# Two feed-forward blocks behind a linear-attention layer: where the first part's splits, weight tiles and tables stand

## The chip, the cores and the metric

One core of a Trainium2 chip runs the whole program in one launch. The metric is the device time of that launch in microseconds (us). The kernel before took 898.88 us, the median of three runs (898.12 to 900.89).

## What is computed

The reference, cut to what matters:

```python
# q, k, v: (4, 8, 768, 64)
for t in range(S):                      # S = 768, gamma per head
    state = gamma * state + outer(k[:, :, t], v[:, :, t])
    y[:, :, t] = scale * q[:, :, t] @ state
x = y in rows of (batch, token), 3072 x 512
h = x @ w_in                            # 512 x 2048
x = (h - tanh(h)) @ w_out               # 2048 x 512
h = x @ w_in2                           # 512 x 1024
solu = h * softmax(h)
out = (layernorm(solu) * g_ln) @ w_out2 # 1024 x 512
```

The weights arrive as 64-bit floats, seen as pairs of 32-bit words. The kernel decodes them into a high and a low 32-bit part, and each product of the feed-forward blocks is made of three matmuls (high by high, high by low, low by high).

## The kernel before

**Units.** The attention is worked in chunks of 128 tokens. A unit is one chunk of one batch entry with all its heads; there are 24, six chunks of four entries, and unit k belongs to chunk k // 4. Each unit has two z parts of 512 KB, with q and k in one and k and v in the other (`load_half`, L192).

`prepare` (L213 to L237) makes a unit's scaled q and v in a tile `vq`: GpSimd (POOL) multiplies q by a table of decays (`qs`, L223) and half of the heads of v by constants (L234); ScalarE (ACT) scales the other four heads (L230). The table `tab` is one for each chunk, 256 KB, in two buffers (`load_tab`, L188).

`unit(ko, ks)` (L240 to L316) does two things: the output of unit `ko` and the scores and states of unit `ks`. On TensorE (PE) the output is `out` products from the states `sa`, `sb` and the masked scores `pr`; the scores are `sc` products, which land in the same tile as the state's gain. All of these are 64x64 matmuls at L211. ACT then copies the output to `xf` (L277, or L280 and L281 in the first chunk), VectorE (DVE) adds the second piece (L285), and `split_x` (L318) makes the high part `xh` on ACT (L323) and the low part `xl` on DVE and POOL (L324). For unit `ks`, DVE masks the scores into `pr` (L305), ACT or DVE makes the state `sb` (L311, L313), and DVE makes the next chunk's state `sa` (L316).

**Weight tiles.** A w_in tile is loaded by SyncE (SP) at L120 and decoded in three stages: an Abs on ACT into `wf` (L126), four steps on DVE (L133, L134, L137, L140), and the split into high and low parts `w`, a cast on ACT (L149) and a subtraction on DVE (L150).

**Order.** The first part works the eight units of the first two chunks: units 0 and 1 are prepared and scored, then a loop over k does the output of unit k beside the scores of unit k + 2, with unit k + 3 prepared in the middle (`ahead`). In the last two rounds the first products `ph` of the feed-forward block (L337) join. From there on PE works 128x512 matmuls to the end. Each engine, and SP's queue of loads, works its instructions in order. `pin` keeps an instruction in program order; one that isn't pinned is put where a scheduler sees fit when the program is built. The loads are not pinned.

```python
def load_tab(c):
    tb[c] = stp.tile([P, NP * P], F32, tag="tab", name="tab", bufs=2)
    (nc.sync if c else nc.scalar).dma_start(out=tb[c], in_=tab[c])
```

Of the kernel before, what the change touches and what calls it, by code (L numbers as in the profile page):

```python
# [26 lines left out]
F32 = mybir.dt.float32  # L27
F32R = mybir.dt.float32r
I32 = mybir.dt.int32
AF = mybir.ActivationFunctionType  # L30
# [5 lines left out]
B, H, S, D = 4, 8, 768, 64  # L36
P = 128
# [10 lines left out]
LAG = 2  # L48
LATER = 3
LOADS = 3  # L50
N4, N2 = 44, 15


W_MIN, W_MAX = (
# [7 lines left out]
C_IDENT = C_MASK + D  # L62
# [28 lines left out]
def body(ctx: ExitStack, tc, z, w_in, w_out, w_in2, w_out2, g_ln, cst, tab, out):  # L91
    nc = tc.nc
# [7 lines left out]
    def pin(ins, on=True):  # L100

        if on:
            tc.keep_in_program_order(ins)
# [7 lines left out]
    con = cpool.tile([P, C_IDENT], F32, name="con")  # L111
# [75 lines left out]

    def load_tab(c):  # L188
        tb[c] = stp.tile([P, NP * P], F32, tag="tab", name="tab", bufs=2)
        (nc.sync if c else nc.scalar).dma_start(out=tb[c], in_=tab[c])  # L190

    def load_half(k, half):  # L192
        t = t4([P, 2, NP, P], F32, "z")
        nc.sync.dma_start(out=t.rearrange("p a b c -> p (a b c)"), in_=z[2 * k + half])
        (zv if half else zq)[k] = t

    def load_units(upto):
        while loaded[0] < min(upto, NU):
            k = loaded[0]
            if k // B not in tb:  # L200
                load_tab(k // B)
            for half in range(2):
                load_half(k, half)
            loaded[0] += 1
# [8 lines left out]
    def prepare(k, own, wide=False):  # L213

        c = k // B
        if wide:
            t = t4([P, 2, H * D], F32, "vq")
            v = t[:, 0, :].rearrange("q (h d) -> q h d", h=H)
            qs[k] = t[:, 1, :].rearrange("q (p t) -> q p t", p=NP)
        else:  # L220
            v = t2([P, H, D], F32, "vs")
            qs[k] = t2([P, NP, P], F32, "qs")
        pin(nc.gpsimd.tensor_tensor(  # L223
            qs[k].rearrange("q p t -> q (p t)"),
            zq[k][:, 0, :, :].rearrange("q p t -> q (p t)"), tb[c], ALU.mult,
        ), wide)
        src = zv[k][:, 1, :, :].rearrange("q p (h d) -> q (p h) d", h=2)
        c0 = C_VS + c * H
        for h in range(own):
            pin(nc.scalar.activation(  # L230
                v[:, h, :], src[:, h, :], AF.Copy, scale=con[:, c0 + h : c0 + h + 1]
            ), wide)
        if own < H:
            pin(nc.gpsimd.tensor_tensor(  # L234
                v[:, own:, :], src[:, own:, :],
                con[:, c0 + own : c0 + H].unsqueeze(2).to_broadcast([P, H - own, D]), ALU.mult,
            ), wide)  # L237
        vs[k] = v

    def unit(ko, ks, hold=False, pool=ps_r, tag="r", engs=None, amid=None):  # L240

        if ko is not None:
            c, b = divmod(ko, B)
            q, v, po, st = qs.pop(ko), vs.pop(ko), pt.pop(ko), (sa.pop(ko, None), sb.pop(ko))
            w = [ps_r.tile([P, 2, 4 * D], F32, tag="r", name="out") for _ in range(2)]
            fr = [t[:, 0, :].rearrange("q (i t) -> q i t", i=2) for t in w]
            y = [t[:, 1, :].rearrange("q (h i t) -> q h i t", h=2, i=2) for t in w]  # L250

            steps = range(2) if c else (1,)
            products([
                (
                    fr[h][rows(col(2 * i + odd, h)), i, rows(ab)],
                    st[ab][rows(h), 2 * i + odd, :], q[rows(h), 2 * i + odd, rows(ab)],
                )
                for i in range(2) for ab in steps for odd in range(2) for h in range(2)
            ])
            products([  # L260
                (
                    y[ab][rows(col(p, h)), h, p // 2, :], v[rows(ab), 2 * p + h, :],
                    po[rows(ab), h, p, :],
                )
                for p in range(NP) for ab in range(2) for h in range(2)
            ])
            if hold:
                if b % 2 == 0:
                    xc[b // 2] = t4([P, 2, 2, 2, P], F32, "xc")
                xf = xc[b // 2][:, b % 2, :, :, :]  # L270
            else:
                xf = t2([P, 2, 2, P], F32, "xf")
            xa = xf.rearrange("q h i t -> q (h i) t")
            ya = [t.rearrange("q h i t -> q (h i) t") for t in y]
            if c:
                for h in range(2):
                    pin(nc.scalar.copy(xf[:, h, :, :], fr[h]), amid)  # L277
            else:
                for h in range(2):
                    pin(nc.scalar.copy(xf[:, h, :, rows(1)], fr[h][:, :, rows(1)]), amid)  # L280
                pin(nc.scalar.copy(xa[:, :, rows(0)], ya[0]), amid)  # L281
            if amid:
                amid()
            for ab in steps:
                pin(nc.vector.tensor_tensor(  # L285
                    xa[:, :, rows(ab)], xa[:, :, rows(ab)], ya[ab], ALU.add
                ), amid)
            if not hold:
                split_x(c, b, xf, engs or (nc.gpsimd, nc.gpsimd), amid)
        if ks is not None:  # L290
            c = ks // B
            kt, kv, v, q = zq.pop(ks)[:, 1, :, :], zv.pop(ks), vs[ks], qs[ks]
            w = [pool.tile([P, 2, 4 * D], F32, tag=tag, name="sc") for _ in range(2)]
            sc, gn = ([t[:, n, :].rearrange("q (p t) -> q p t", p=NP) for t in w] for n in range(2))
            products([
                (sc[h][rows(ab), p, :], kt[rows(h), p, rows(ab)], q[rows(h), p, rows(ab)])
                for p in range(NP) for h in range(2) for ab in range(2)
            ])
            products([
                (gn[ab][rows(h), p, :], kv[rows(ab), 0, p, rows(h)], v[rows(ab), 2 * p + h, :])  # L300
                for p in range(NP) for ab in range(2) for h in range(2)
            ])
            pr = t2([P, 2, NP, D], F32, "pr")
            for h in range(2):
                pin(nc.vector.tensor_tensor(  # L305
                    pr[:, h, :, :], sc[h], mask.unsqueeze(1).to_broadcast([P, NP, D]), ALU.mult
                ), amid)
            pt[ks] = pr
            sb[ks] = stp.tile([P, NP, D], F32, tag="sb", name="sb", bufs=3)
            if c == 0:  # L310
                nc.scalar.copy(sb[ks], gn[0])  # L311
            else:
                nc.vector.tensor_tensor(sb[ks], sa[ks], gn[0], ALU.add)  # L313
            if c < NC - 1:
                sa[ks + B] = stp.tile([P, NP, D], F32, tag="sa", name="sa")
                nc.vector.tensor_tensor(sa[ks + B], sb[ks], gn[1], ALU.add)  # L316

    def split_x(c, b, xf, engs, fixed=False):  # L318
        if b == 0:
            xt[c] = [[t4([P, 2, SB], F32R, f"x{n}") for _ in range(2)] for n in "hl"]  # L320
        for h in range(2):
            xh, xl = (xt[c][n][h][:, :, b * P : (b + 1) * P] for n in range(2))
            pin(nc.scalar.copy(xh, xf[:, h, :, :]), fixed)  # L323
            pin(engs[h].tensor_tensor(xl, xf[:, h, :, :], xh.bitcast(F32), ALU.subtract), fixed)  # L324
# [75 lines left out]

    spare = dict(pool=ps_y, tag="y")
    dec1.n = NF1

    warm = cpool.tile([P, 1], F32, name="warm")
    nc.gpsimd.memset(warm, 0.0)
    nc.scalar.activation(warm, warm, AF.Tanh)
    g2 = {}

    def step_h(n, b):
# [3 lines left out]

    load_half(0, 0)
    load_tab(0)
    nc.scalar.dma_start(out=con, in_=cst[:, :C_IDENT])
    load_half(0, 1)
    loaded[0] = 1
    load_units(2)
    dec1.to(0, 2)  # L420
    load_units(2 * B)
    for k in range(2):
        prepare(k, H // 2, True)
        unit(None, k, **spare)
    for st in (1, 2):
        dec1.to(st, 1, True)
    prepare(2, H // 2, True)

    def ahead(k):
# [3 lines left out]
    for k in range(2 * B):  # L433
        both = (nc.vector, nc.gpsimd) if k < 2 * B - 1 else (nc.vector, nc.vector)
        unit(
            k, k + 2 if k + 2 < 2 * B else None, engs=both,
            amid=lambda: ahead(k + 3), **spare
        )

        if k == 0:  # L440
            for st, n in ((3, 1), (1, 2), (2, 2)):
                dec1.to(st, n, True)
        elif k == 1:
            dec1.to(3, 2, True)
        elif k >= 2 * B - 2:
            if k == 2 * B - 1:
                dec1.to(0, 4)
                for st in (1, 2, 3):
                    dec1.to(st, 3, True)
            step_h(k - (2 * B - 2), 0)  # L450
# [241 lines left out]
```

## Time and profile before

| | us |
|---|---|
| median of three runs | 898.88 |
| lowest and highest run | 898.12, 900.89 |
| the profiled execution | 900.99 |
| its span, first to last instruction | 899.2 |
| PE busy | 874.1 |
| DVE busy | 434.1 |
| ACT busy | 301.4 |
| POOL busy | 193.8 |

The span is what the trace covers; the profiled execution's own time has 1.8 us around it. The trace can be read as totals, as busy time in chosen stretches, or as a timeline of one engine's instructions, each with the idle time ahead of it and what ended that. "Issue" there stands for idle time in which the engine waited for nothing that the profile shows. [...]

### The profile page before, as it was taken

What the parts mean: (1) busy time and instruction counts of PE and PEld (TensorE: products, weight loads), DVE (VectorE), ACT (ScalarE), POOL (GpSimd) and SP (SyncE); (2) the same over time, 40 slices, a digit from 0 to 9 for tenths busy, and PEclk for the clock granted to TensorE, in tenths of its full rate; (3) what the DMA queues carried; (4) which work ended last, traced back from release to release, by engine and by line L of the source; (5) the groups of instructions that cost most, each with busy time, mean ns of one, the idle gap of its engine ahead of it and who ended that gap; (6) DMA issues with size and microseconds to landing.
All of it is one profiled execution on the core that took longest, in us unless ns stands there. A gap on an engine that the chain in (4) does not pass through costs nothing.

```text
span 899.2 us, 15890 instructions
## 1 busy us (share of the span) xinstructions
PE 874.1 (97%) x6656; PEld 723.5 (80%) x6656; DVE 434.1 (48%) x873; ACT 301.4 (34%) x606; POOL 193.8 (22%) x200
## 2 busy tenths in 40 slices
PE   4699999999999999999999999999999999999998
PEld 4588888888888887888788888888888888888886
DVE  3679759981232232222222279954444444444442
ACT  4556436550111111111111134523444433333332
POOL 4411000000234333333333200011222212122210
PEclk8799999999999999999999999999999999999999
DMA  9663105340321112111310055114111111100000
GB/s 359 251 265 130 48 1 187 95 140 0 94 95 48 60 64 79 48 47 48 95 48 14 12 183 150 43 41 123 47 48 40 35 44 47 36 24 24 24 24 35
DMA packets 34775, 71.93 MB, mean 80 GB/s; under 512 B 3088, under 2 KB 15504, under 8 KB 34704
## 3 DMA queue, kind: packets, MB, share of 16 engines
q1 hardware_dynamic: 18288, 58.01, 19.0%
q10 hardware_dynamic: 16416, 12.91, 4.5%
q8 instruction: 52, 0.85, 0.4%
q14 instruction: 19, 0.16, 0.1%
HBM read 58.32 MB, written 12.58 MB: 79 GB/s over the span
## 4 chain that ended last, share of the span: by engine, by line
PE 94%; DMA 2%; issue 1%; DVE 1%; ACT 1%; POOL 1%; ACTq 0%; POOLq 0%
PE ph L337 29%; PE py L362 29%; PE po L616 15%; PE ph L568 15%; PE out L211 3%; PE ptr L603 2%; PE sc L211 2%; DMA z<-z 1%; DMA con<-cst 1%; DMA y1d<-ysb 0%; POOL qs L223 0%; POOL vs L234 0%; DVE g L345 0%; ACT th L344 0%; DVE w L150 0%
## 5 line engine op out<-in xcount | busy, mean ns | idle before, releaser
L362 PE MATMUL py<-gh,w 128*128 128x512 f32 x768 | 248.8, 392 | 0.0
L337 PE MATMUL ph<-xh,w 128*128 128x512 f32 x768 | 247.9, 393 | 0.0
L337 PEld LDWEIGHTS ph<-xh,w 128*128 128x128 f32 x768 | 145.3, 189 | 31.0
L362 PEld LDWEIGHTS py<-gh,w 128*128 128x128 f32 x768 | 143.3, 188 | 30.4 <-ACT gh L350 0.2
L345 DVE TENSOR_TENSOR g<-ph,th 128x512 f32<-128x512 f32 x96 | 66.2, 690 | 182.3 <-ACT th L344 182.3
L337 PE MATMUL ph<-xl,w 128*128 128x512 f32 x384 | 150.4, 392 | 0.0
L362 PE MATMUL py<-gl,w 128*128 128x512 f32 x384 | 149.8, 390 | 0.0
L344 ACT ACTIVATE th<-ph 128x512 f32<-128x512 f32 x96 | 57.3, 598 | 258.9 <-PE ph L337 245.9
L568 PE MATMUL ph<-w,y 128*128 128x512 f32 x576 | 134.9, 389 | 0.0
L353 POOL TENSOR_TENSOR gl<-g,gh 128x512 fp32r<-128x512 f32 x48 | 61.9, 1289 | 331.6 <-DVE gh L352 298.0
L568 PEld LDWEIGHTS ph<-w,y 128*128 128x128 f32 x576 | 108.0, 188 | 22.4
L616 PE MATMUL po<-w,uh 128*128 128x512 f32 x384 | 120.4, 395 | 0.0
L397 POOL TENSOR_TENSOR y<-yl,y 128x512 fp32r<-128x512 f32 x24 | 42.2, 1761 | 260.9 <-ACT y L396 260.9
L574 DVE TENSOR_REDUCE nmx<-ph 128x1 f32<-128x1024 f32 x24 | 29.4, 1225 | 117.7 <-PE ph L568 117.7
L337 PEld LDWEIGHTS ph<-xl,w 128*128 128x128 f32 x384 | 72.6, 189 | 14.9
L362 PEld LDWEIGHTS py<-gl,w 128*128 128x128 f32 x384 | 72.1, 188 | 14.9
L616 PEld LDWEIGHTS po<-w,uh 128*128 128x128 f32 x384 | 70.6, 188 | 13.6
L616 PE MATMUL po<-w,ul 128*128 128x512 f32 x192 | 75.3, 392 | 0.0
L577 ACT ACTIVATE ex<-ph,nmx 128x1024 f32<-128x1024 f32 x24 | 26.8, 1117 | 132.5 <-DVE nmx L574 132.5
L579 DVE SCALAR_TENSOR_TENSOR ex<-ph,ex 128x1024 f32<-128x1024 f32 x24 | 29.4, 1225 | 29.8 <-ACT ex L577 29.8
L616 PEld LDWEIGHTS po<-w,ul 128*128 128x128 f32 x192 | 36.0, 188 | 7.6
L353 DVE TENSOR_TENSOR gl<-g,gh 128x512 fp32r<-128x512 f32 x48 | 33.8, 707 | 10.1 <-PE py L362 8.1
(76 smaller groups left out, 840.4 us busy)
## 6 DMA issues: line engine op xcount, KB each, us to landing
z<-z SPq DMA_DIRECT2D x48, 512.0 KB, 5.3
raw<-w_in SPq DMA_DIRECT2D x24, 512.0 KB, 5.2
raw<-w_out SPq DMA_DIRECT2D x24, 512.0 KB, 3.7
y1d<-ysb ACTq DMA_DIRECT2D x24, 256.0 KB, 3.5
yl<-y1d SPq DMA_DIRECT2D x24, 256.0 KB, 3.2
out<-ob ACTq DMA_DIRECT2D x24, 256.0 KB, 2.2
tab<-tab SPq DMA_DIRECT2D x5, 256.0 KB, 2.6
tab<-tab ACTq DMA_DIRECT2D x1, 256.0 KB, 4.7
```

Of the source, the lines that this page charges most:

```text
L211: pin(nc.tensor.matmul(o, a, b, start=True, stop=True, skip_group_check=True))
L337: nc.tensor.matmul(ph, a[:, k, :], x, start=n == 0, stop=n == 3 * NK - 1), s < 2
L344: nc.scalar.activation(th, ph, AF.Tanh)
L345: nc.vector.tensor_tensor(g, ph, th, ALU.subtract)
L353: eng_l.tensor_tensor(gl_, g, gh.bitcast(F32), ALU.subtract)
L362: nc.tensor.matmul(py[e], a[:, cols], x, start=f == 0 and n == 0, stop=f == NF1 - 1 and n == 2)
L397: nc.gpsimd.tensor_tensor(yo, t, yh.bitcast(F32), ALU.subtract)
L568: nc.tensor.matmul(ph[:, half, :], a[:, k, :], b, start=n == 0, stop=n == 3 * NK - 1)
L574: nc.vector.tensor_reduce(nmx, phf, AX.X, ALU.max, negate=True)
L577: nc.scalar.activation(ex, phf, AF.Exp, bias=nmx, scale=1.0, accum_out=ssum)
L579: nc.vector.scalar_tensor_tensor(ex, phf, 1.0, ex, ALU.mult, ALU.mult, accum_out=us)
L616: nc.tensor.matmul(po, a[:, f, :], b, start=n == 0, stop=n == 3 * NF2 - 1)
```

## The change

Five things change, all in the first part:

- `split_x` of unit k (the making of `xh` and `xl`) is called behind the scores and states of unit k + 2, at the end of `unit`, instead of ahead of them.
- The first two w_in tiles are loaded directly behind unit 0's two z parts, ahead of unit 1's, and decoded around unit 1's scores: tile 0 between the scores of units 0 and 1, tile 1 behind them. Before, they were decoded ahead of and inside the loop's first two rounds.
- The loads of the tables are pinned, so they stay in program order on SP.
- The load of the constants is pinned and stands ahead of the tiny activation that loads ACT's table.
- ACT's copy of the first chunk's `sb` is pinned.

```diff
@@ load_tab
-        (nc.sync if c else nc.scalar).dma_start(out=tb[c], in_=tab[c])
+        pin((nc.sync if c else nc.scalar).dma_start(out=tb[c], in_=tab[c]))
@@ unit
-            if not hold:
-                split_x(c, b, xf, engs or (nc.gpsimd, nc.gpsimd), amid)
+            if not hold and not amid:
+                split_x(c, b, xf, engs or (nc.gpsimd, nc.gpsimd))
...
             if c == 0:
-                nc.scalar.copy(sb[ks], gn[0])
+                pin(nc.scalar.copy(sb[ks], gn[0]))
             else:
                 nc.vector.tensor_tensor(sb[ks], sa[ks], gn[0], ALU.add)
             if c < NC - 1:
                 sa[ks + B] = stp.tile([P, NP, D], F32, tag="sa", name="sa")
                 nc.vector.tensor_tensor(sa[ks + B], sb[ks], gn[1], ALU.add)
+        if amid:
+            split_x(*divmod(ko, B), xf, engs, True)
@@ body
-    warm = cpool.tile([P, 1], F32, name="warm")
-    nc.gpsimd.memset(warm, 0.0)
-    nc.scalar.activation(warm, warm, AF.Tanh)
...
     load_half(0, 0)
     load_tab(0)
-    nc.scalar.dma_start(out=con, in_=cst[:, :C_IDENT])
+    pin(nc.scalar.dma_start(out=con, in_=cst[:, :C_IDENT]))
     load_half(0, 1)
+
+    warm = cpool.tile([P, 1], F32, name="warm")
+    nc.gpsimd.memset(warm, 0.0)
+    pin(nc.scalar.activation(warm, warm, AF.Tanh))
     loaded[0] = 1
-    load_units(2)
     dec1.to(0, 2)
     load_units(2 * B)
-    for k in range(2):
-        prepare(k, H // 2, True)
-        unit(None, k, **spare)
-    for st in (1, 2):
-        dec1.to(st, 1, True)
+    prepare(0, H // 2, True)
+    unit(None, 0, **spare)
+    for st, n in ((1, 1), (2, 1), (1, 2)):
+        dec1.to(st, n, True)
+    prepare(1, H // 2, True)
+    dec1.to(3, 1, True)
+    unit(None, 1, **spare)
+    for st in (2, 3):
+        dec1.to(st, 2, True)
     prepare(2, H // 2, True)
...
-        if k == 0:
-            for st, n in ((3, 1), (1, 2), (2, 2)):
-                dec1.to(st, n, True)
-        elif k == 1:
-            dec1.to(3, 2, True)
-        elif k >= 2 * B - 2:
+        if k >= 2 * B - 2:
```

How the order of the built program moves, at three places. The first is SP's queue of loads, up to the weight tiles behind the second chunk's z parts; `tab` are the tables (the load of the first one stands on ACT). Before:

```order
L194 DMA z<-z 128x1024 x4
L120 DMA raw<-w_in 128x1024 x2
L194 DMA z<-z 128x1024 x4
L190 DMA tab<-tab 128x512
L194 DMA z<-z 128x1024 x8
L451 DMA gl<-g_ln 128x8
L557 DMA ident<-cst 128x128
L190 DMA tab<-tab 128x512 x2
L120 DMA raw<-w_in 128x1024 x5
L194 DMA z<-z 128x1024 x4
L120 DMA raw<-w_in 128x1024
```

With the change:

```order
L194 DMA z<-z 128x1024 x2
L120 DMA raw<-w_in 128x1024 x2
L194 DMA z<-z 128x1024 x6
L190 DMA tab<-tab 128x512
L194 DMA z<-z 128x1024 x8
L451 DMA gl<-g_ln 128x8
L557 DMA ident<-cst 128x128
L120 DMA raw<-w_in 128x1024 x5
L190 DMA tab<-tab 128x512
L194 DMA z<-z 128x1024 x4
L120 DMA raw<-w_in 128x1024
```

The two w_in tiles now pass unit 1's z parts. Of the two tables that stood ahead of five w_in tiles, the one of chunk 2 stands behind them and the one of chunk 3 has gone further down, behind the last w_out tile.

The second place is ACT, from unit 0's scaling to unit 2's. `vq_127` is unit 0's; unit 1's is `vq_175` before and `vq_183` with the change; unit 2's is `vq_229` and `vq_241`. Before:

```order
L230 ACTIVATE vq_127<-z_91,con_69 128x64 x4
L311 COPY sb_171<-sc_134 128x256
L230 ACTIVATE vq_175<-z_95,con_69 128x64 x4
L311 COPY sb_219<-sc_182 128x256
L126 ACTIVATE wf_223<-raw_97 128x512
L230 ACTIVATE vq_229<-z_103,con_69 128x64 x4
```

With the change:

```order
L230 ACTIVATE vq_127<-z_88,con_69 128x64 x4
L311 COPY sb_171<-sc_134 128x256
L126 ACTIVATE wf_175<-raw_93 128x512
L126 ACTIVATE wf_181<-raw_95 128x512
L230 ACTIVATE vq_183<-z_99,con_69 128x64 x4
L149 CAST w_190<-wf_175 128x512
L311 COPY sb_230<-sc_193 128x256
L149 CAST w_238<-wf_181 128x512
L230 ACTIVATE vq_241<-z_103,con_69 128x64 x4
```

Both tiles' Abs and both casts now stand ahead of unit 2's scaling.

The third place is DVE, from unit 0's state to unit 2's scores (`pr_316` before, `pr_320` with the change). Before:

```order
L316 TENSOR_TENSOR sa_173<-sb_171,sc_135 128x256
L305 TENSOR_TENSOR pr_216<-sc_182,con_69 128x256
L305 TENSOR_TENSOR pr_216<-sc_183,con_69 128x256
L316 TENSOR_TENSOR sa_221<-sb_219,sc_183 128x256
L133 TENSOR_SCALAR wf_223<-wf_223 128x512
L134 TENSOR_SCALAR wf_223<-wf_223 128x512
L137 SCALAR_TENSOR_TENSOR wf_223<-raw_97,wf_223 128x512
L140 SCALAR_TENSOR_TENSOR wf_223<-raw_97,wf_223 128x512
L285 TENSOR_TENSOR xf_262<-xf_262,out_237 128x4x64
L324 TENSOR_TENSOR xl_276<-xf_262,xh_274 128x2x128
L305 TENSOR_TENSOR pr_316<-sc_282,con_69 128x256
```

With the change, from behind unit 0's state (`sa_173`, as before) into the decode of tile 1:

```order
L133 TENSOR_SCALAR wf_175<-wf_175 128x512
L134 TENSOR_SCALAR wf_175<-wf_175 128x512
L137 SCALAR_TENSOR_TENSOR wf_175<-raw_93,wf_175 128x512
L140 SCALAR_TENSOR_TENSOR wf_175<-raw_93,wf_175 128x512
L150 TENSOR_TENSOR w_190<-wf_175,w_190 128x512
L305 TENSOR_TENSOR pr_227<-sc_193,con_69 128x256
L305 TENSOR_TENSOR pr_227<-sc_194,con_69 128x256
L316 TENSOR_TENSOR sa_232<-sb_230,sc_194 128x256
L133 TENSOR_SCALAR wf_181<-wf_181 128x512
L134 TENSOR_SCALAR wf_181<-wf_181 128x512
```

and, behind tile 1's decode, unit 0's parts of x around unit 2's scores:

```order
L150 TENSOR_TENSOR w_238<-wf_181,w_238 128x512
L285 TENSOR_TENSOR xf_274<-xf_274,out_249 128x4x64
L305 TENSOR_TENSOR pr_320<-sc_286,con_69 128x256
L305 TENSOR_TENSOR pr_320<-sc_287,con_69 128x256
L316 TENSOR_TENSOR sa_325<-sb_323,sc_287 128x256
L326 TENSOR_TENSOR xl_329<-xf_274,xh_327 128x2x128
```

Unit 1's scores (`pr_216` before, `pr_227` now) stand behind the whole decode of tile 0, and unit 0's `xl` (L326 now) has gone from ahead of unit 2's `pr` to behind its state. PE's order and POOL's order are the same in both programs.

## Rows read from the trace of the kernel before

**Rows 1.** The page, parts 1 and 3: totals by engine, and the instruction queue.
```profile
PE 874.1 (97%) x6656; PEld 723.5 (80%) x6656; DVE 434.1 (48%) x873; ACT 301.4 (34%) x606; POOL 193.8 (22%) x200
...
q8 instruction: 52, 0.85, 0.4%
```

**Rows 2.** Busy us by stretch: length, PE, PEld, DVE, ACT, POOL, granted clock, DMA share, GB/s.
```profile
50.00:75.00 25.00, 25.00 (x170) 20.54 (x169) 23.62 (x44) 16.15 (x40) 3.59 (x2) 1.00 0.39 156
325.00:350.00 25.00, 24.39 (x226) 19.99 (x225) 7.94 (x16) 4.79 (x11) 8.85 (x8) 1.00 0.41 127
425.00:450.00 25.00, 24.39 (x225) 20.03 (x224) 7.61 (x15) 4.93 (x10) 8.67 (x9) 1.00 0.34 112
```

**Rows 3.** PE's timeline, first part: start us, us, instruction, [idle time before, what ended it].
```profile
16.14 1.52 PE L211 MATMUL sc<-vq,z 64*64 64x64 f32 x29 [0.16 <-ACT vq L230]
...
22.52 0.28 PE L211 MATMUL sc<-vq,z 64*64 64x64 f32 x3 [1.89 <-issue]
...
27.32 0.38 PE L211 MATMUL out<-vq,sb 64*64 64x64 f32 x9 [2.82 <-ACT sb L311]
...
28.87 0.38 PE L211 MATMUL out<-vq,sb 64*64 64x64 f32 x4 [1.16 <-issue]
...
35.96 0.27 PE L211 MATMUL out<-vq,sa 64*64 64x64 f32 x1 [0.41 <-issue]
...
41.95 0.37 PE L211 MATMUL out<-vq,sa 64*64 64x64 f32 x2 [3.87 <-issue]
...
43.43 0.79 PE L337 MATMUL ph<-xh,w 128*128 128x512 f32 x1
```

**Rows 4.** Busy us by stretch, cut where PE's "issue" waits end.
```profile
22.50:28.86 6.36, 2.38 (x127) 2.10 (x126) 5.53 (x11) 3.69 (x15) 2.96 (x4) 0.91 0.93 357
28.86:35.95 7.09, 6.60 (x253) 6.28 (x253) 5.14 (x15) 5.50 (x22) 5.71 (x7) 0.60 0.06 17
35.95:41.94 5.99, 2.13 (x126) 1.99 (x127) 4.16 (x12) 1.67 (x6) 1.46 (x2) 0.95 0.99 340
41.94:48.16 6.22, 6.21 (x55) 5.12 (x55) 1.18 (x3) 1.36 (x4) 1.16 (x2) 0.50 1.02 406
48.16:54.99 6.83, 6.83 (x89) 5.49 (x89) 4.49 (x10) 3.14 (x8) 0.85 (x1) 1.00 1.03 410
```

**Rows 5.** SP's timeline: issues of loads.
```profile
22.88 12.28 SPq L190 DMA_DIRECT2D tab<-tab  x2
35.21 2.33 SPq L120 DMA_DIRECT2D raw<-w_in  x5
37.66 3.19 SPq L194 DMA_DIRECT2D z<-z  x4
```

**Rows 6.** Timeline of POOL, DVE and ACT, 8 to 22.6 us.
```profile
8.18 1.27 POOL L223 TENSOR_TENSOR vq<-z,tab 128x512 f32<-128x512 f32 x1 [0.29 <-DMA z<-z]
9.28 0.76 DVE L305 TENSOR_TENSOR pr<-sc,con 128x256 f32<-128x256 f32 x2 [9.28 <-PE sc L211]
10.15 0.42 DVE L316 TENSOR_TENSOR sa<-sb,sc 128x256 f32<-128x256 f32 x1
...
12.45 0.66 ACT L126 ACTIVATE wf<-raw 128x512 f32<-128x512 f32 x1
...
13.15 0.43 DVE L133 TENSOR_SCALAR wf<-wf 128x512 f32<-128x512 f32 x1
13.61 1.37 DVE L134 TENSOR_SCALAR wf<-wf 128x512 int32<-128x512 int32 x1
...
15.01 0.69 DVE L137 SCALAR_TENSOR_TENSOR wf<-raw,wf 128x512 int32<-128x512 int32 x1
...
15.74 1.06 ACT L230 ACTIVATE vq<-z,con 128x64 f32<-128x64 f32 x4 [2.63 <-DMA z<-z]
...
20.77 0.62 ACT L149 CAST w<-wf 128x512 fp32r<-128x512 f32 x1
...
21.43 1.15 DVE L150 TENSOR_TENSOR w<-wf,w 128x512 fp32r<-128x512 f32 x1
```

## The prediction

> **What bounds the kernel now.** I read the page's totals first: TensorE (PE) is busy 874.1 of 899.2 us [rows 1], so only PE's idle time and its slow clock can be won or added to. The table of stretches shows where that idle time lies. From 50 to 75 us PE is busy 25.00 of 25, and the later stretches read the same; the two exceptions lose 0.61 us each [rows 2]. So the end moves with the start of PE's unbroken run, which is at 41.95 us. What stands ahead of 41.95 is the first part, the scores and states of eight units of attention, and nothing behind it has slack to absorb a shift.
>
> PE's timeline before 41.95 says what it waits for. One wait is for an engine: 2.82 us for ScalarE's copy `sb` at 27.32. Four are marked "issue", where no semaphore is late: 1.89, 1.16, 0.41 and 3.87 us, 7.33 us in all [rows 3]. The last one sits in the middle of a unit's output products, right ahead of the unbroken run. I read them as waits for instructions. PE has 6656 matmuls and 6656 weight loads, 13,312 instructions, and queue q8, the instruction queue, moves 52 packets and 0.85 MB [rows 1]: 13,312 / 52 = 256 instructions of 64 B in each packet. Between the ends of the "issue" waits PE ran 127, 253 and 126 matmuls [rows 4]. 126 matmuls with their weight loads and a few semaphores are one packet, 253 are two. So PE stops where a packet ends and the next is not there.
>
> What a packet costs depends on the other transfers. With the DMA engines busy (share 0.93 and 0.99) a packet took 6.36 and 5.99 us from end of wait to end of wait; with them idle (share 0.06) two took 7.09, that is 3.55 each [rows 4]. PE worked only 2.38 and 2.13 us of the first two. **While transfers run, PE is fed 126 matmuls every 6.0 us**; one unit's scores and outputs are 128.
>
> Why were the transfers idle in between? SyncE (SP) issued two `tab` loads over 12.28 us, from 22.88, and only then, at 35.21, five `w_in` tiles [rows 5]. The second of them (the table of units 12 to 15) waits for a buffer that GpSimd (POOL) frees with unit 7's product, and everything behind it on SP's queue waits too. This gave PE two cheap packets. When the loads came back at 35.21, the 3.87 us wait followed.
>
> **The change, part by part.** PE's own order is the same in both programs, so every term is about when PE is fed and released.
>
> (1) *Tables in program order.* On SP the five `w_in` loads now follow `ident` directly, then the table of units 8 to 11, then the z parts. The stop of 12.28 us is gone. What follows is 5 + 1 + 1 + 1 `w_in` tiles and 8 z parts of 512 KB and a table of half that. At the 406 to 410 GB/s of the last stretches [rows 4] 512 KB take 1.28 us, so these 16.5 pieces take 21 us. The transfers before them end near 28.9 (share 0.06 from there on [rows 4]), so the queue now stays full to about 50 us. Hence the two cheap packets become dear ones: 2 x 5.99 - 7.09 = **+4.9 us**. The packet that took 6.36 had PE's 2.82 us wait for `sb` in it [rows 3]; at the plain price it takes 5.99: **-0.4 us**.
>
> (2) *First two w_in tiles behind unit 0's z.* Their loads pass unit 1's z parts on SP: 2 x 1.28 us later, the parts land near 10.7 and 12.0 rather than 8.2 and 9.4 (POOL's product for unit 1 starts at 8.18 on landing [rows 6]). This is covered, since unit 2's z, which lands as before, sets the next step. The order on ScalarE (ACT) is not covered. Unit 2's four copies `vq`, at 15.74 in the trace on landing, now stand behind the cast L149 of the second w_in tile. That cast needs VectorE's four decode steps of tile 1, which stand behind unit 1's `pr` and `sa`, which stand behind tile 0's decode. From the rows [rows 6]: VectorE is free at 10.57 (10.15 + 0.42); ACT's Abs (0.66) ends near 10.8; four decode steps take 0.43 + 0.43 + 0.69 + 0.69 = 2.24, or 3.18 where the second one takes 1.37; the cast 0.62; the low part L150 0.69 to 1.15; `pr` 0.76 and `sa` 0.42; four steps again; the cast 0.62. The sum is 18.4 at the low end and 20.7 at the high end, so `vq` is 2.7 to 5.0 us late. I take **+3.5**: in the trace one step of four was held, not every long one. PE's first packet of the chain is asked for in the middle of these products (16.14, 29 of them on `vq` [rows 3]), 126 matmuls ahead of the wait that ended at 22.52, so the delay is passed on to every later packet and is not made up while packets are 6 us apart.
>
> (3) *Parts of x behind the next scores and states.* On VectorE `xl` goes behind `pr`, `sb` and `sa`. It no longer waits for ACT's cast in front of them. It could remove up to all of the 2.82 us for `sb`. I cost it at **nothing**: PE gets 126 matmuls in 6.0 us and waits for instructions, which covers it. If that cover is gone, it is worth up to 2.8 us.
>
> (4) *Constants ahead of the activation table, pins on small copies; the later tables.* Nothing: the constants feed unit 0, whose work is covered by the later `vq`; the later tables load long before use, and PE is full there [rows 2].
>
> [...]
>
> Sum: 3.5 + 4.9 - 0.4 = **+8.0 us**. The unbroken run starts near 50 instead of 41.95. The profiled execution took 900.99 us (span 899.2 and 1.8 around it), so 909.0; it lay 2.1 above the median of the runs, and from the median 898.88 it is **906.9 us**. This case's own range: 2.7 or 5.0 for the late `vq` and 3.1 either way for the clock, not all at one end, give +4 to +10.5, or 902.9 to 909.4.
>
> **Rivals.** *A, faster: the feed of instructions doesn't follow the transfers.* Then the "issue" waits stay as they are and the engines' chain decides, where (3) removes up to the whole 2.82 us [rows 3]: 898.88 - 2.8 = **896.1 us**. It decides if the late `vq` is made up before 27.32, that is if packets arrive in time. For it: the waits carry no named cause. Against it: 126, 253 and 126 matmuls, and the price that follows the DMA share. [...]
>
> *B, slower by less: the transfers run dry again.* The loads behind the fifth w_in tile wait for buffers that units free. If SP finds them late, the last two packets ahead of the run cost 3.55 each: 8.0 - 4.9 = +3.1, **902.0 us**. For it: in the changed order those loads name PE, VectorE, ACT and POOL as releasers, and PE is late. Against: the buffers they wait for are those of the first units, read long before.
>
> *C, no change.* The gain of (3) and one dear packet (2.4) cancel, with `vq` late but made up: within 2.7 us of 898.9. That the change doesn't do what it says I leave out: the order shows all three moves.
>
> **How the numbers follow.** Chances: the forecast 0.68, B 0.14, A 0.11, C 0.07. A measurement of this kernel tells about 0.3%, 2.7 us, from no change. The forecast and B are slower by more: 0.82; A 0.11; C 0.07. The range runs from just under B to the top of the forecast's own: 901.0 to 910.0, leaving out A, C and the tails.
>
> **What would show it.** Right: SP's w_in loads from 22.9 on without a stop; DMA share near 1 from 25 to past 45; "issue" waits of 2 to 4 us on PE that recur about 6 us apart up to 50; unit 2's `vq` on ACT near 19; the first `ph` of L337 (L339 now) near 51 instead of 43.43 [rows 3]. Wrong: `ph` before 43 or no "issue" waits after 30 (A); a DMA share near 0 between 33 and 45 (B); a half-clock stretch after the start that is gone or twice as long (the size).

## The result and the profile after

The changed kernel takes **907.76 us** (median of 4 runs, 907.18 to 908.43) against 899.88 us for the kernel before (4 runs, 898.12 to 901.15): a ratio of 1.0089 [1.0067, 1.0111], **slower by 7.9 us**. The forecast was 906.9. The profiled execution took 907.18 us, with a span of 905.4.

The totals of the page, part 1, hardly move: PE's busy time is 0.5 us under that of [rows 1], and the instruction queue moved the same 52 packets.

```profile
PE 873.6 (96%) x6656; PEld 724.1 (80%) x6656; DVE 435.2 (48%) x873; ACT 301.1 (33%) x606; POOL 193.1 (21%) x200
```

The loss lies at the front. Busy us by stretch, the columns as in [rows 2]:

```profile
50.00:75.00 25.00, 24.57 (x234) 20.19 (x226) 20.79 (x42) 14.25 (x34) 5.28 (x5) 0.99 0.20 63
325.00:350.00 25.00, 24.40 (x269) 19.86 (x271) 8.13 (x17) 4.93 (x10) 9.17 (x9) 1.00 0.28 85
425.00:450.00 25.00, 24.39 (x224) 20.02 (x225) 8.70 (x18) 4.93 (x10) 9.02 (x9) 1.00 0.31 97
```

The two later stretches lose what they lost before. The first now loses 0.43 us, because the first part reaches into it. PE's timeline, to be read against [rows 3]:

```profile
22.30 1.52 PE L211 MATMUL sc<-vq,z 64*64 64x64 f32 x29 [5.81 <-ACT vq L230]
...
28.70 0.28 PE L211 MATMUL sc<-vq,z 64*64 64x64 f32 x3 [2.02 <-issue]
...
41.01 0.26 PE L211 MATMUL out<-vq,sa 64*64 64x64 f32 x1 [2.54 <-issue]
...
47.08 0.37 PE L211 MATMUL out<-vq,sa 64*64 64x64 f32 x1 [2.38 <-issue]
...
51.09 0.27 PE L211 MATMUL out<-vq,sa 64*64 64x64 f32 x2 [0.43 <-issue]
...
51.94 0.50 PE L339 MATMUL ph<-xh,w 128*128 128x512 f32 x1
```

PE's wait for unit 2's `vq` has grown from 0.16 to 5.81 us, and the product behind it starts 6.16 us later. The wait for `sb` is gone; behind 22.30 all waits are marked "issue", five of them (the one not shown ends at 34.78) where there were four. The unbroken run starts at 51.09 instead of 41.95, and `ph` at 51.94 instead of 43.43. Cut where these waits end (columns as in [rows 4]), the packets read:

```profile
28.70:34.78 6.08, 2.77 (x127) 2.58 (x126) 4.03 (x10) 3.15 (x12) 4.25 (x5) 0.60 1.03 405
34.78:41.01 6.23, 3.68 (x127) 3.50 (x128) 2.17 (x6) 2.26 (x9) 3.43 (x5) 0.50 1.03 408
41.01:47.08 6.07, 3.69 (x128) 3.50 (x127) 2.50 (x7) 2.23 (x8) 1.01 (x2) 0.50 1.03 406
47.08:51.09 4.01, 3.58 (x126) 3.44 (x127) 1.65 (x5) 1.36 (x4) 0.29 (x1) 0.59 0.88 291
51.09:57.31 6.22, 6.22 (x126) 5.09 (x126) 3.15 (x9) 2.61 (x7) 2.40 (x3) 1.00 0.12 47
```

Three packets of 6.07 to 6.23 us with the DMA share at 1.03, then one of 4.01 us at 0.88, in which the transfers end. [Rows 4] had two dear ones with the two cheap ones between. The last line is new in another way: the run starts at the granted clock 1.00 (TensorE's, as a share of its full speed), where the same place stood at 0.50 before. SP's queue, against [rows 5]:

```profile
23.02 5.54 SPq L120 DMA_DIRECT2D raw<-w_in  x5
29.51 0.33 SPq L190 DMA_DIRECT2D tab<-tab  x1
29.94 2.69 SPq L194 DMA_DIRECT2D z<-z  x4
...
42.45 14.13 SPq L120 DMA_DIRECT2D raw<-w_in  x3
```

The stop of 12.28 us is gone, and the w_in loads go out from 23.02. A new stop stands further down: the three w_in loads from 42.45 take 14.13 us to go out, while SP waits, 13.4 us of it for VectorE's decode step L140. So what is queued runs out, and the DMA share falls from 0.96 (45 to 50 us) to 0.28 (50 to 55).

**Where the 6.2 us of span went** (905.4 - 899.2): `vq` +6.2; the four packets behind it 22.39 us (28.70 to 51.09) where they took 19.43 (22.52 to 41.95), +3.0; together the start of the run, +9.1. The remaining -2.9 I put down to the clock: the first 6.22 us of the run had a granted clock of 0.50 [rows 4] and have 1.00 now, which I estimate to be worth up to 3.1, half of the 6.22. The medians differ by 7.9 because the profiled execution of before lay 1.1 us above its median (900.99 and 899.88) and that of after 0.6 below.

### The profile page after: what moved, and what is told of

Same layout as the page of the kernel before. It is cut to its first block, busy times and chain, and to the rows that moved or that the text cites. A ratio compares the mean times of both kernels' runs of the same rounds, so it can differ in the third digit from the quotient of the medians.

```text
span 905.4 us, 15895 instructions
## 1 busy us (share of the span) xinstructions
PE 873.6 (96%) x6656; PEld 724.1 (80%) x6656; DVE 435.2 (48%) x873; ACT 301.1 (33%) x606; POOL 193.1 (21%) x200
## 4 chain that ended last, share of the span: by engine, by line
PE 95%; issue 2%; DVE 1%; POOL 1%; DMA 1%; ACT 1%; POOLq 0%; ACTq 0%
PE ph L339 29%; PE py L364 29%; PE po L616 15%; PE ph L568 14%; PE sc L211 3%; PE out L211 3%; PE ptr L603 2%; DMA tab<-tab 1%; POOL qs L223 0%; DVE wf L140 0%; POOL vs L234 0%; DVE wf L134 0%; DVE w L150 0%; DVE wf L137 0%; DVE g L347 0%
## 5 line engine op out<-in xcount | busy, mean ns | idle before, releaser
L149 ACT CAST w<-wf 128x512 fp32r<-128x512 f32 x48 | 29.7, 618 | 29.7 <-DVE wf L140 29.6
```

The costliest lines, as they stand in the source:

```text
L149: pin(nc.scalar.copy(hi, wf), fixed)
```

## The experiments

Experiments 1 to 4 were timed beside one set of runs of the kernel before (900.26 us, 15 runs), 5 to 8 beside a second (898.99, 28 runs), 9 and 10 beside a third (899.24, 15 runs). I compare by the ratio to the kernel before of the same set. Line numbers below are each kernel's own; `sc` and `out` are the same products at L211 or L215.

**1. The tables alone.** The kernel before with the tables pinned in program order; the constants' load and the tiny activation move with them.

```diff
-        (nc.sync if c else nc.scalar).dma_start(out=tb[c], in_=tab[c])
+        pin((nc.sync if c else nc.scalar).dma_start(out=tb[c], in_=tab[c]))
...
-    nc.scalar.activation(warm, warm, AF.Tanh)
...
-    nc.scalar.dma_start(out=con, in_=cst[:, :C_IDENT])
+    pin(nc.scalar.dma_start(out=con, in_=cst[:, :C_IDENT]))
...
+    pin(nc.scalar.activation(warm, warm, AF.Tanh))
```

> Before with the change's loads alone: tables pinned in program order, constants pinned ahead of the table load; w_in tiles and x as before. Engine orders on PE, DVE and POOL are as before; on SP the five w_in tiles follow ident without a stop. Feed theory (a packet of 126 matmuls takes 6.0 us while transfers run, 3.5 with none): unit 2's vq stays near 15.7, the issue waits end near 22.5, 28.9, 35, 41 and 47, and PE's unbroken run starts near 47 instead of 41.95: +4.9 us, 903 to 907 with 3.1 either way for the clock at most. Engine-chain theory (issue waits do not follow the transfers, only the late vq costs): run start near 42, time within 1 us of before.

Measured: 906.57 us, ratio 1.0076 [1.0063, 1.0089]. `vq` comes in time (PE starts on it at 16.44), and between 22.65 and 47.35 all four packets are dear. Busy us by stretch of this kernel:

```profile
22.65:28.85 6.20, 3.45 (x129) 3.08 (x128) 5.37 (x11) 3.54 (x14) 2.79 (x4) 0.56 1.03 402
28.85:35.07 6.22, 3.68 (x126) 3.49 (x127) 4.70 (x13) 3.79 (x15) 5.41 (x7) 0.50 1.03 402
35.07:41.14 6.07, 3.69 (x127) 3.50 (x127) 2.50 (x7) 2.23 (x8) 1.32 (x3) 0.50 1.03 408
41.14:47.35 6.21, 3.35 (x127) 3.21 (x128) 2.50 (x7) 1.36 (x4) 0.73 (x1) 0.77 1.03 407
```

They take 24.70 us where the same four took 19.43 [rows 3]: the run starts 5.4 us later. So the change's loads alone cost 6.3 us by the medians, most of the whole. No run has the tables without the constants' load and the activation; but experiments 5 to 7 keep those two moves and lose nothing, so the cost is not theirs.

**2. The two w_in tiles alone.** The kernel before with the tiles loaded behind unit 0's z and decoded around unit 1's scores, as in the change; tables and x stay.

```diff
-    load_units(2)
     dec1.to(0, 2)
     load_units(2 * B)
-    for k in range(2):
-        prepare(k, H // 2, True)
-        unit(None, k, **spare)
...
+    prepare(0, H // 2, True)
+    unit(None, 0, **spare)
+    for st, n in ((1, 1), (2, 1), (1, 2)):
+        dec1.to(st, n, True)
+    prepare(1, H // 2, True)
...
```

> Before with the first two w_in tiles alone moved: loaded behind unit 0's z and decoded around unit 1's scores; tables and x as before, so SP's stop is back. Unit 2's vq near 22 as in the changed kernel, 6 us late. Feed theory: the delay is largely made up, because the packets behind the one at 28.7 find few transfers under way and take 3.5 to 4 us: run start 42.5 to 44.5, time -1 to +3 us against before. Engine-chain theory: the 6 us of the late vq stay to the end, +5 to +6 us.

Measured: 904.02 us, 1.0049 [1.0034, 1.0064]. PE starts on `vq` at 22.57, 6.4 us late, yet the time grows by only 3.8. That lies between the two theories' ranges: the feed theory, which is mine, gave -1 to +3 us and a run start at 42.5 to 44.5, and the run started at 47.33. SP's old stop is still there, and longer:

```profile
23.33 15.19 SPq L190 DMA_DIRECT2D tab<-tab  x2
38.58 3.44 SPq L120 DMA_DIRECT2D raw<-w_in  x5
```

Busy us by stretch of this kernel:

```profile
28.84:33.01 4.17, 2.11 (x129) 1.97 (x128) 2.66 (x8) 2.53 (x10) 3.00 (x5) 1.00 0.06 18
33.01:36.85 3.84, 2.88 (x126) 2.69 (x127) 2.03 (x6) 2.26 (x9) 2.39 (x3) 0.64 0.02 4
36.85:40.73 3.88, 3.69 (x128) 3.50 (x127) 2.03 (x7) 2.24 (x8) 2.06 (x4) 0.50 0.42 87
40.73:47.33 6.60, 2.19 (x126) 2.05 (x127) 3.73 (x11) 1.36 (x4) 1.29 (x2) 0.99 0.95 365
```

The transfers are idle from about 29 in both kernels, so a later `vq` moves one more packet into the quiet. But the last packet, with the loads back, takes 6.60 us. By the start of the run 1.0 us of the 6.4 is made up (47.33 is 5.4 behind 41.95); that my sum had excluded, but it is less than I expected here. The rest of the difference may be the clock, 0.72 in the first 6.17 us of this run and 0.50 in the kernel before; no run tests that.

**3. Parts of x behind, alone.** The pin on ACT's copy `sb` goes with it.

```diff
-            if not hold:
-                split_x(c, b, xf, engs or (nc.gpsimd, nc.gpsimd), amid)
+            if not hold and not amid:
+                split_x(c, b, xf, engs or (nc.gpsimd, nc.gpsimd))
...
-                nc.scalar.copy(sb[ks], gn[0])
+                pin(nc.scalar.copy(sb[ks], gn[0]))
...
+        if amid:
+            split_x(*divmod(ko, B), xf, engs, True)
```

> Before with the parts of x alone moved behind the next scores and states (and the copy of sb pinned). Feed theory: PE waits for instructions there, so the shorter VectorE chain is covered: within 1.5 us of before, the 2.82 us wait for sb smaller and the issue wait behind it longer by as much. Engine-chain theory: the 2.82 us are saved, 896 us.

Measured: 900.18 us, 1.0000 [0.9991, 1.0009]. PE's timeline of this kernel:

```profile
26.86 0.38 PE L211 MATMUL out<-vq,sb 64*64 64x64 f32 x9 [0.85 <-ACT sb L311]
...
29.06 0.38 PE L211 MATMUL out<-vq,sb 64*64 64x64 f32 x4 [1.81 <-issue]
```

The wait for `sb` fell from 2.82 to 0.85 us, and the next "issue" wait grew from 1.16 to 1.81 and ends at 29.06 instead of 28.87 [rows 3]. So the stretch ended 0.19 us later, though PE's wait for an engine ahead of it was 1.97 us shorter: I read its end as the packet's arrival.

**4. Transfers that nobody reads.** The kernel before with five copies of 512 KB from memory to memory, issued on SP behind the second chunk's z; no instruction waits for them.

```diff
     load_units(2 * B)
+    for i in range(5):
+        spare_d = yd.tile([P, 1024], F32, name=f"spare{i}")
+        nc.sync.dma_start(out=spare_d, in_=z[i])
```

> Before with five copies of 512 KB from z to memory that nothing reads, issued on SP behind the second chunk's z parts, so that they fill the stretch in which the DMA engines stood idle; nothing else is changed, and no engine reads what they move. Feed theory: the DMA share between 29 and 35 goes from 0.06 to near 1, one or two of the packets there go from 3.5 to 6 us, and the run starts 2 to 5 us later: +1 to +5 us. Engine-chain theory: no change, within 1 us.

Measured: 904.52 us, 1.0061 [1.0045, 1.0077]. PE's timeline:

```profile
28.80 0.38 PE L211 MATMUL out<-vq,sb 64*64 64x64 f32 x4 [1.18 <-issue]
...
35.03 0.21 PE L211 MATMUL out<-vq,sa 64*64 64x64 f32 x1 [2.73 <-issue]
...
39.53 0.27 PE L211 MATMUL out<-vq,sa 64*64 64x64 f32 x1 [1.05 <-issue]
...
45.53 0.33 PE L211 MATMUL out<-vq,sa 64*64 64x64 f32 x2 [3.87 <-issue]
```

Busy us by stretch:

```profile
28.80:35.03 6.23, 3.50 (x126) 3.36 (x127) 4.37 (x13) 3.56 (x13) 5.43 (x7) 0.75 0.88 328
35.03:39.53 4.50, 3.45 (x127) 3.26 (x127) 2.14 (x7) 2.24 (x8) 0.98 (x2) 0.62 0.86 293
```

The packet from 28.80 takes 6.23 us and the next 4.50, together 10.73 where 7.09 stood at a DMA share of 0.06 [rows 4]. No engine waits for these copies; they only occupy the transfers. The w_in loads go out at 35.12, as before (35.21 [rows 5]), so it isn't their place that makes the packets dear. This shows that transfers in flight make PE's packets late, here by 3.64 us over two packets. How late is not a matter of the mean share alone, which is nearly the same in the two lines (0.88 and 0.86).

**5. The changed kernel without the transfers.** The other side of the same claim: the changed kernel, whose w_in tiles from the third and z of units 8 to 11 may start only when the sixth unit is done (behind that unit's work POOL writes one element in each partition of the buffer, and the load must wait for the write).

```diff
         raw = t4([P, 512, 2], I32, "raw")
+        if wait:
+            pin(nc.gpsimd.memset(raw[:, 0, :1], 0))
...
-                    self.raw[i] = raw_load(self.srcs[i])
+                    self.raw[i] = raw_load(self.srcs[i], self is dec1 and i in (2, 3, 4, 5, 6, 7, 8))
...
         t = t4([P, 2, NP, P], F32, "z")
+        if k in (8, 9, 10, 11):
+            pin(nc.gpsimd.memset(t[:, 0, 0, :1], 0.0))
...
+        if k == 5:
+            dec1.to(0, 5)
```

> The changed kernel with its later loads held back: the w_in tiles from the third of the first part and z of units 8 to 11 start only behind the sixth unit's work, so that from about 24 us no transfer is in flight for a while; everything else is the changed kernel's. Feed theory (an instruction packet takes some 6.0 us under full transfers and about 3.5 us beside none): the packets that come behind 29 us are cheap again, the table wait of unit 2's vq stays (ends about 22), ph comes at 43 to 45 instead of 51.9, so 896 to 901 us, even with or below the kernel before. Rival (the packets are dear because of what SP issues before them, that is the order of the tables, and not because of transfers in flight): the packets stay at 6 us and the time stays at 905 to 909.

Measured: 899.97 us, 1.0008 [0.9998, 1.0019]. Busy us by stretch:

```profile
28.04:31.38 3.34, 2.11 (x129) 1.97 (x128) 2.74 (x8) 2.58 (x11) 1.52 (x2) 1.00 0.05 15
31.38:34.95 3.57, 2.10 (x127) 1.96 (x128) 3.52 (x9) 2.82 (x11) 3.57 (x5) 1.00 0.03 7
34.95:38.80 3.85, 2.11 (x127) 1.97 (x126) 2.71 (x8) 2.23 (x8) 3.47 (x5) 1.00 0.03 6
38.80:42.60 3.80, 2.13 (x126) 1.99 (x127) 2.56 (x8) 1.36 (x4) 0.66 (x2) 1.00 0.02 4
```

The same PE instructions in the same order, with the DMA share at 0.02 to 0.05: four packets in 14.56 us instead of 22.39. The late `vq` is still there (the wait is 5.74 us), and the loss of the change is gone, to within the 0.2% of the interval.

**6 and 7. The kernel before with the loads held.** Both have the tables in program order, and the w_in tiles where the kernel before has them, with the holds of experiment 5; one with the parts of x behind, one with them ahead.

```diff
+        pin((nc.sync if c else nc.scalar).dma_start(out=tb[c], in_=tab[c]))
...
+            pin(nc.gpsimd.memset(raw[:, 0, :1], 0))
...
+        if k == 5:
+            dec1.to(0, 5)
```

> The kernel before with x put behind, the tables in program order, the w_in tiles where they were, and the same loads held back till the sixth unit. Feed theory: all packets behind the first are cheap (3.4 to 4.0 us each), and the vq of unit 2 comes at its time; ph comes at 39 to 41 instead of 43.4, so 893 to 897 us, under both kernels. Rival (the first part is bound by the chain of vector and activation steps, the packets only show in its gaps): 898 to 902.

> As the run before it, with x converted ahead of the scores as in the kernel before. Feed theory: with cheap packets the issue waits still end behind the wait for the softmax copy that x delays, so x's place still hides: within 0.2% of the run before it, 893 to 897. Rival (with cheap packets the copy's 2.8 us become the bound): 1 to 3 us slower than the run before it.

The "softmax copy" of the last expectation is ACT's copy `sb`; there is no softmax in this part.

Measured: x behind 896.24 us, 0.9963 [0.9949, 0.9977]; x ahead 897.13 us, 0.9975 [0.9964, 0.9985]. **Both are faster than the kernel before**, and the first has the lowest median of the study, 1.25% under the changed kernel by the two ratios (0.9963 / 1.0089). Busy us by stretch of the first:

```profile
22.33:28.41 6.08, 2.37 (x127) 2.10 (x126) 5.50 (x11) 3.05 (x13) 2.59 (x4) 0.95 0.86 332
28.41:32.03 3.62, 3.36 (x127) 3.22 (x128) 2.83 (x9) 3.38 (x14) 3.62 (x5) 0.61 0.05 15
32.03:35.33 3.30, 2.11 (x127) 1.97 (x126) 3.30 (x10) 2.26 (x9) 3.30 (x6) 1.00 0.02 5
35.33:38.59 3.26, 2.13 (x127) 1.99 (x128) 2.63 (x8) 1.36 (x4) 0.72 (x2) 1.00 0.02 5
38.59:44.81 6.22, 6.22 (x126) 5.09 (x126) 3.35 (x9) 2.60 (x7) 1.71 (x11) 1.00 0.69 188
```

All three packets from 28.41 on are cheap, the run starts at 38.59, 3.4 us earlier than before, and at a granted clock of 1.00. PE gives back 0.97 us between 55 and 75, where it is busy 19.03 of 20 and waits for VectorE's `w` of later tiles. The two kernels' intervals overlap, so these runs don't show what the place of x is worth once the feed is cheap.

**8. The two w_in tiles in the middle.** As experiment 6, with their loads behind the fifth unit's z and their decode at units 1 and 2.

```diff
-    load_units(2)
+    load_units(5)
     dec1.to(0, 2)
...
+        if k in (1, 2):
+            for st in (1, 2, 3):
+                dec1.to(st, 1 + (k == 2), True)
```

> As the second run of this batch, with the first two w_in tiles loaded behind the fifth unit's z and converted at units 1 and 2 instead of 0 and 1. Feed theory: the same cheap packets and a vector engine that is free earlier: 0 to 2 us below the second run, 892 to 896. Rival (the conversions beside units 1 and 2 put the tanh and vq steps off): 1 to 4 us above it.

Measured: 899.22 us, 1.0000 [0.9988, 1.0012]. My theory missed here and the rival held: 3 us over experiment 6. PE's timeline has a wait for an engine where there was none:

```profile
37.14 1.51 PE L215 MATMUL sc<-vq,z 64*64 64x64 f32 x29 [3.20 <-ACT vq L234]
```

With cheap packets PE is close to the engines' chain, and the decode put in front of this `vq` shows as a wait of 3.20 us.

**9. POOL out of the way of the decode.** Why was `vq` later than the 2.7 to 5.0 us of my bounds? In the changed kernel VectorE's steps of the first w_in tile are long where POOL works beside them. VectorE's timeline:

```profile
11.34 1.37 DVE L134 TENSOR_SCALAR wf<-wf 128x512 int32<-128x512 int32 x1
12.74 0.98 DVE L137 SCALAR_TENSOR_TENSOR wf<-raw,wf 128x512 int32<-128x512 int32 x1
13.76 1.64 DVE L140 SCALAR_TENSOR_TENSOR wf<-raw,wf 128x512 int32<-128x512 int32 x1
16.08 1.76 DVE L150 TENSOR_TENSOR w<-wf,w 128x512 fp32r<-128x512 f32 x1 [0.68 <-ACT w L149]
...
20.66 0.69 DVE L140 SCALAR_TENSOR_TENSOR wf<-raw,wf 128x512 int32<-128x512 int32 x1
```

and POOL's:

```profile
10.91 1.51 POOL L223 TENSOR_TENSOR vq<-z,tab 128x512 f32<-128x512 f32 x1 [2.85 <-DMA z<-z]
...
13.47 1.38 POOL L223 TENSOR_TENSOR vq<-z,tab 128x512 f32<-128x512 f32 x1 [0.29 <-DMA z<-z]
...
16.03 1.26 POOL L223 TENSOR_TENSOR vq<-z,tab 128x512 f32<-128x512 f32 x1 [0.16 <-DMA z<-z]
```

L140 took 0.69 us for the second tile, with POOL idle, and 1.64 for the first. It started at 13.76, inside POOL's product of 13.47 to 14.85, and ended at 15.40, 0.55 us behind that product's end. L150 started at 16.08, 0.05 us behind the start of a POOL product, and ended 0.55 behind its end at 17.29. L134 and L137 of the first tile, 1.37 and 0.98 us where the second tile took 0.43 and 0.69, stand beside POOL too. The experiment puts one tiny POOL operation that reads the second tile's decoded words ahead of unit 2's products on POOL:

```diff
-    for st in (2, 3):
-        dec1.to(st, 2, True)
+    dec1.to(2, 2, True)
+    gate = cpool.tile([P, 1], F32, name="gate")
+    pin(nc.gpsimd.tensor_tensor(gate, dec1.wf[1][:, :1], dec1.wf[1][:, :1], ALU.add))
+    dec1.to(3, 2, True)
     prepare(2, H // 2, True)
```

> The changed kernel with one POOL operation of 128x1 that reads the second w_in tile's decoded words, ahead of unit 2's products on POOL: POOL's products of units 2 and 3 (L223, L234) start only when VectorE's decode steps of the second tile are done. Theory (VectorE's steps of the first tile are slow because POOL works beside them): the step L140 at 13.76 falls from 1.64 to about 0.69, L150 at 16.08 from 1.76 to about 0.7, and ACT's vq starts about 2 us earlier, near 20 instead of 21.90; PE's products on it wait then for POOL's own late product and start at 20.5 to 22.0, so the time is 905 to 908 us. Rival (these steps are long for another reason, such as the transfers that land meanwhile): L140 and L150 stay at 1.6 to 1.8 with POOL idle beside them and vq stays near 22.

Measured: 907.53 us, 1.0092 [1.0077, 1.0107]. VectorE's timeline:

```profile
13.56 0.69 DVE L140 SCALAR_TENSOR_TENSOR wf<-raw,wf 128x512 int32<-128x512 int32 x1
14.94 0.69 DVE L150 TENSOR_TENSOR w<-wf,w 128x512 fp32r<-128x512 f32 x1 [0.68 <-ACT w L149]
...
19.76 1.35 DVE L150 TENSOR_TENSOR w<-wf,w 128x512 fp32r<-128x512 f32 x1 [0.68 <-ACT w L149]
```

The two steps fell to 0.69 us, and L150 of the second tile, now beside POOL's product of 19.30, rose to 1.35: the long steps are the ones that POOL works beside. At two places the one that started first kept its time. POOL's product of 16.03 took 1.26 us with L150 starting 0.05 behind it, as against 1.27 with VectorE idle (at 8.18 [rows 6]); and in the kernel before L140 started at 15.73 and took 0.69, while POOL's L234, which started 0.06 behind it, took 1.11 where it took 0.61 with VectorE idle (at 18.37). Why the two hold each other up isn't shown by these runs.

ACT's `vq` came 2.3 us earlier (19.63). PE gained 1.7 of them, since it then waits for POOL's own late product:

```profile
20.62 2.05 PE L211 MATMUL sc<-vq,z 64*64 64x64 f32 x63 [5.07 <-POOL vq L223]
```

And yet nothing was won. The packets' waits end at 27.44, 33.52, 39.75, 46.10 and 51.21: the one that took 4.01 us now takes 5.11, by my reading since more of it lies in the transfers (it begins at 46.10 instead of 47.08, and the DMA share is 0.97 from 45 to 50), and the run starts at 51.21 instead of 51.09.

**10. The hold one unit shorter.** As experiment 6, held till the fifth unit.

```diff
-        if k == 5:
+        if k == 4:
             dec1.to(0, 5)
```

> As the run of the kernel before with the loads held till the sixth unit, but held till the fifth only, so some 3 us earlier. Feed theory: the last packet ahead of ph overlaps the transfers again and costs 4.5 to 6 us instead of 3.3 (+1.2 to +2.7), while VectorE's w for the third tile is earlier and gives back up to the 1.0 us that PE waited for it between 55 and 75 us: 896 to 898.5 us, no better than 896.24. Rival (what is left is the late w_in tile): 894.5 to 895.5.

Measured: 896.52 us, 0.9969 [0.9960, 0.9979], the same as experiment 6. The last packet took 3.80 us (35.48 to 39.28) instead of 3.26, less than I expected, and PE lost 0.61 instead of 0.97 us between 55 and 75: the two even out.

## Why the prediction was right, and which terms were not

The direction, the mechanism and the size of the whole held: 906.9 foretold, 907.76 measured. Most marks of the forecast are in the trace: SP's loads from 23.02 without the old stop, a DMA share of 0.96 to 1.04 in every 5 us from 25 to 50, waits for instructions some 6 us apart, `ph` at 51.94. Two are not: unit 2's `vq` on ACT came at 21.90 and not near 19, and the stretch at a granted clock of 0.50 behind the start is gone, which I had named as a sign that the size is wrong. Three terms were mis-sized, and their errors cancel: 6.2 + 3.0 - 2.9 = 6.3 us, the 6.2 of span but for rounding, where I had 3.5 + 4.5 + 0 (for the clock) = 8.0. That the total came within 1 us of the measured time owes something to luck.

- **(1) Tables.** The mechanism is shown from both sides: filler transfers in a quiet stretch make packets dear (10.73 us for two instead of 7.09, experiment 4), and the changed kernel with the transfers held loses nothing (1.0008, experiment 5). For the tables alone the size nearly held: packets +5.3 us in experiment 1 against 4.9 - 0.4. In the whole change it was +3.0, because with `vq` late the last packet is asked for at the end of the transfers and takes 4.01 us. The step that failed is that a late `vq` is "not made up while packets are 6 us apart". The transfers end because SP's queue stops, which hardly follows `vq` (from 40.97 us in experiment 1, where `vq` is in time, and from 42.45 here), and packets that fall into or behind such an end are cheaper (4.01 us here; 3.84 at a DMA share of 0.02 in experiment 2). So (1) and (2) can't be added: the run starts 3.7 us later than in experiment 1 (51.09 and 47.35), not 6.2. Experiments 2 and 9 show it from either side.
- **(2) vq.** +6.2 us, outside my 2.7 to 5.0. I allowed for one held step of four (the 1.37 of [rows 6]); four steps of the first tile took 4.42 us where my high end had 3.18, and L150 1.76 where it had 1.15. Each of the long ones ran beside a product of POOL's (experiment 9). I should have laid POOL's timeline beside the new place of the decode. Nor did the whole +6.2 reach the end: experiment 9 takes 2.3 us of it away on ACT, 1.7 for PE, and the time stays.
- **(3) x.** Nothing, as foretold (experiment 3).
- **(4) Constants, activation, pins.** Nothing foretold, and no run has them alone; experiments 5 to 7 have them and lose nothing.
- **Clock.** -2.9, near one end of the 3.1 us either way in my range. No run shows that 3.1 by itself: it is an estimate, half of the 6.22 us at a granted clock of 0.50 [rows 4]; what the traces show in its place is 0.50 over those 6.22 us before and 1.00 over the first 6.22 us of the run now. For the sum I took the same clock as before, so nothing. In the last three packets ahead of its run PE worked 3.58 to 3.69 us each at clocks of 0.50 to 0.59, where before it had worked 2.13 us of 5.99 at 0.95 [rows 4]; then the run started at 1.00. I had taken the packets ahead of it to be the same. What decides it isn't settled by these runs: experiment 6 starts its run at clock 1.00 behind packets with 2.1 us of work. Nor does one kernel always have the same clock: in the 58 runs of the kernel before that were timed beside the experiments its mean over a run lies between 0.988 and 0.998. The 13 runs at 0.988 have a median of 900.45 us, the 15 at 0.994 or more one of 898.72. The profiled execution had 0.988, so part of the -2.9 may be its own and not the change's.

Rival A (feed and transfers independent) is refuted by experiments 3 and 4. Where PE works 64x64 matmuls, its waits for instructions show even beside a DMA share of 0.05 (experiment 5: PE at work 2.11 of 3.34 us), and more beside full transfers (2.13 of 5.99 us at 0.99 [rows 4]). Where it works 128x512 matmuls none shows in 50 to 75 us, with 25.00 of 25 us busy [rows 2]. Rival B's stop on SP did come, at 42.45, but late: its cheap packets appear only in the last one, at the end of the transfers. Rival C fell with the result.

## What to carry to other kernels

Where an engine works many short instructions, cut its "issue" waits into stretches and count the instructions in each: equal counts (here 126 to 129 of the 64x64 matmuls) suggest that it waits to be fed, and whether the bulk transfers in flight are part of the bound, as they were here, is decided by a test like experiments 4 and 5. Transfers that nothing needed yet were not free here: five copies that nobody reads cost 0.61% (experiment 4), the two kernels that hold later weights back until the short matmuls are done are 0.25 and 0.37% faster than the kernel before, and a queue's accidental stop of 12.28 us [rows 5] had been doing the same service before the change removed it. And when work is moved to a new place, lay beside it what the engine that can hold it up does there, as POOL did to VectorE's decode (L140 took 1.64 us beside it and 0.69 without).

## What I had not expected of the hardware

- 126 to 129 matmuls with their weight loads arrived in 3.26 to 4.17 us beside a DMA share of 0.02 to 0.06 (experiments 2, 5 and 6), and in 5.99 to 6.60 us beside one of 0.86 to 1.12 (the kernel before, the changed kernel, experiments 1 to 4 and 6), also where nobody reads what the transfers move: some 2.5 us more for each packet (6.0 against 3.5), with PE's order unchanged. Two packets in which the transfers let up for a while lie between: 4.01 us at a share of 0.88 (changed kernel) and 4.50 at 0.86 (experiment 4).
- The cheap price is a price too: in experiment 5 PE worked 2.10 to 2.13 of 3.34 to 3.85 us beside a DMA share of 0.02 to 0.05, at a granted clock of 1.00. At 0.50 it was nearly covered: in experiment 2 PE worked 3.69 of 3.88 us, beside a share of 0.42.
- VectorE's decode steps and POOL's products are longer beside each other: L140's 0.69 us became 1.64 and L150's 0.69 became 1.76 (changed kernel), and POOL's L234 took 1.06 us beside L140 (at 14.82, changed kernel) and 0.61 with VectorE idle (at 18.37, kernel before). The 1.37 us of L134 in [rows 6], inside POOL's product of 13.29 to 14.69, is such a one: for the second tile of the changed kernel, with POOL idle, it took 0.43.
